# Packed attention and a gated feed-forward on one core: the first batch's attention with turned queries, scores in parts of the array and a block softmax on VectorE

## The chip, the cores and the metric

One core of one Trainium2 chip runs the whole program. The metric is the time of one execution on the device in microseconds (us), lower is better. The engines are named as the profile names them: PE is TensorE, DVE is VectorE, ACT is ScalarE, POOL is GpSimd and SP is SyncE, whose queue issues all loads and stores.

## What is computed

```python
q, k, v: (8, 8, 576, 64)   p: (8, 8, 32, 64)   w_in: (512, 2048)   w_out: (2048, 512)

def sm_attn(qq, kk, vv):
    s = scale * np.matmul(qq, kk.transpose(0, 1, 3, 2))
    s = s - np.max(s, axis=-1, keepdims=True)
    a = np.exp(s)
    a = a / (np.sum(a, axis=-1, keepdims=True) + 1e-09)
    return np.matmul(a, vv)
p_packed = sm_attn(p, k, v)                # 32 packed rows attend to 576 keys
out = sm_attn(q, p_packed, p_packed)       # 576 queries attend to the 32 packed rows
x = out.transpose(0, 2, 1, 3).reshape(8 * 576, 512)
h = x @ w_in
g = h * np.clip(h + 3.0, 0.0, 6.0) / 6.0
return g @ w_out
```

q, k, v and p arrive as 32-bit floats, the two weights as 64-bit floats, which the kernel reads as pairs of 32-bit words.

## The kernel before

Attention and feed-forward are done batch by batch, 576 rows each. The second attention's weights `a` (576 queries by 8 heads of 32) are never multiplied with the packed values. Instead the packed values are multiplied with w_in, which gives `m` for each strip `f` of 128 hidden columns (16 strips), and the hidden row is `a` times `m`. Numbers that must keep their precision are split into a rounded part `hi` and the remainder `lo`, and a product is then three matmuls: hi with hi, lo with hi, hi with lo.

For one strip f, first_moe does this: `gemm1` (12 matmuls into `h`), an activation on ACT (`t`, L954), the gate on DVE (L955), the rounding to `gh` on ACT (L963), the remainder `gl` on POOL (L965), and twelve matmuls of `second_product` (L856) into four accumulators, one strip later.

The weights of a strip come as 64-bit floats and are narrowed in a chain of four: two activations on ACT (L142, L144), a shift on DVE (L148), an addition on POOL (L152). w_in(f) is then ready for `m`; w_out(f) goes on to a rounding `wo_hi` on ACT (L162) and a remainder `wo_lo` on DVE or POOL (L164). The raw weights have two buffers for each matrix, and a buffer is free for the next load when POOL has added.

The first batch's attention (`first_attention`) has nothing to lie behind, so its pieces are written out by hand as generators, and `step` and `rest` move each on by one or more of its `yield`s: `b0` and `b1` are the second scores, softmax and split of head group 0 and 1 (`s2`), `m0` and `m1` are m of strip 0 and 1, `win0`, `wout0`, `win1`, ... are the narrowings. The order in which these calls stand is the order of the instructions on PE, DVE, ACT and POOL, and each engine works its queue strictly in that order. This holds for the attention of the first batch and for strips 0 to 3 of the feed-forward; after that a scheduler sets the order. `warm(n)` issues n matmuls on zeros whose result nobody reads.

In `s2` before, the queries are the stationary operand: the scores of 128 queries stand on 128 partitions with 32 packed rows of each head side by side. The softmax runs along the free axis straight from PSUM (L663, L666, L667, L670), and PE then turns the weights (L692, L695) into PSUM, from where ACT rounds them to `a_hi` (L698) and DVE takes the remainder `a_lo` (L701).

## Time and profile before

| | |
|---|---|
| three timed runs | 761.15, 763.76, 763.96 us; median 763.76 us |
| the profiled execution | 758.97 us, of which 757.1 us from the first to the last instruction |
| busy in the span | PE 98%, ACT 51%, DVE 44%, POOL 37% |
| instructions | 13994 |

A busy time is the time in which an engine works on something; matmuls overlap each other, and their ends are modelled. The granted clock is the share of full speed that TensorE was given. The two levels are 2.4 GHz (1.0) and 1.2 GHz (0.5).

### The profile page before, as it was taken

To read this page: it belongs to the slowest core of one execution; us is meant where nothing else is said; L and a number is where in the kernel's file an instruction comes from. 1 tells how busy PE (TensorE), PEld (TensorE's weight loads), DVE (VectorE), ACT (ScalarE), POOL (GpSimd) and SP (SyncE) were. 2 spreads that over 40 slices of the span, in tenths; PEclk is the share of its full clock that TensorE was granted. 3 is DMA by queue.
4 is the path that set the end of the run, shared out by engine and by line. 5 is a ranking of instruction groups with operands and counts; after the bars stand their busy time and mean duration, and the time that the engine had idled before them with its cause. 6 is when DMAs were issued, how large, how long until landed. Compare 5 with 4: busy or idle time off the path is not lost.

```text
span 757.1 us, 13994 instructions
## 1 busy us (share of the span) xinstructions
PE 739.4 (98%) x5197; PEld 583.4 (77%) x5197; DVE 336.3 (44%) x709; ACT 387.6 (51%) x922; POOL 282.3 (37%) x420
## 2 busy tenths in 40 slices
PE   8998898999999999999999999999999999999998
PEld 6775675768777877888777886788787887888886
DVE  3676648432463355342733446342643527321121
ACT  4677864644455446463455535463354635553343
POOL 0487973423233233332333223333333333343332
PEclk9999899999999999999999999999999999999999
DMA  9859983104420532043310524024220210000010
GB/s 257 261 144 218 237 223 63 56 9 88 102 37 29 103 67 52 1 88 71 63 43 1 114 53 82 1 58 98 47 61 1 61 33 29 1 29 0 2 42 29
DMA packets 191205, 55.98 MB, mean 74 GB/s; under 512 B 173216, under 2 KB 184480, under 8 KB 191136
## 3 DMA queue, kind: packets, MB, share of 16 engines
q1 hardware_dynamic: 191136, 55.08, 31.6%
q8 instruction: 41, 0.67, 0.4%
q14 instruction: 28, 0.23, 0.1%
HBM read 45.61 MB, written 9.44 MB: 73 GB/s over the span
## 4 chain that ended last, share of the span: by engine, by line
PE 83%; DMA 5%; DVE 4%; SPq 3%; ACT 3%; issue 1%; POOL 1%; DVEq 0%; POOLq 0%; ACTq 0%
PE acc L856 47%; PE ps_hh L827 23%; PE ps L268 6%; SPq L216 2%; DMA raw_in<-in_moe_w_in_dram 2%; PE ps L323 2%; DMA nat<-in_k_dram 1%; PE ps_h L451 1%; DVE tr L401 1%; PE ps L307 1%; SPq L254 1%; POOL x_out L152 1%; PE ps_w L639 1%; DMA raw_out<-in_moe_w_out_dram 1%; DMA spare<-in_k_dram 1%
## 5 line engine op out<-in xcount | busy, mean ns | idle before, releaser
L845 POOL TENSOR_TENSOR g<-t,g 128x256 fp32r<-128x256 f32 x224 | 167.5, 751 | 410.7 <-ACT g L844 384.5
L856 PE MATMUL acc<-wo_hi,g 128*128 128x512 f32 x896 | 316.4, 394 | 1.3 <-ACT g L844 1.3
L840 DVE SCALAR_TENSOR_TENSOR t<-t,ps_hh 128x320 f32<-128x320 f32 (+1 forms) x224 | 100.1, 449 | 251.8 <-ACT t L839 251.6
L839 ACT ACTIVATE t<-ps_hh,three 128x320 f32<-128x320 f32 (+1 forms) x224 | 112.4, 503 | 177.9 <-PE ps_hh L827 169.8
L856 PEld LDWEIGHTS acc<-wo_hi,g 128*128 128x128 f32 x896 | 167.7, 188 | 35.4 <-issue 3.5
L856 PE MATMUL acc<-wo_lo,g 128*128 128x512 f32 x448 | 177.6, 396 | 0.0
L844 ACT CAST g<-t 128x256 fp32r<-128x256 f32 x224 | 90.4, 405 | 93.9 <-DVE t L840 92.6
L827 PE MATMUL ps_hh<-a_hi,m_hi 128*128 128x320 f32 (+1 forms) x448 | 136.2, 304 | 0.3 <-DVE t L840 0.3
L827 PE MATMUL ps_hh<-a_lo,m_hi 128*128 128x320 f32 (+1 forms) x448 | 132.7, 296 | 0.0
L827 PE MATMUL ps_hh<-a_hi,m_lo 128*128 128x320 f32 (+1 forms) x448 | 132.7, 296 | 0.0
L827 PEld LDWEIGHTS ps_hh<-a_hi,m_hi 128*128 128x128 f32 x448 | 84.4, 188 | 34.4 <-issue 19.9
L856 PEld LDWEIGHTS acc<-wo_lo,g 128*128 128x128 f32 x448 | 84.5, 189 | 12.4 <-issue 2.1
L827 PEld LDWEIGHTS ps_hh<-a_lo,m_hi 128*128 128x128 f32 x448 | 84.5, 189 | 8.2 <-issue 0.9
L827 PEld LDWEIGHTS ps_hh<-a_hi,m_lo 128*128 128x128 f32 x448 | 84.5, 189 | 1.6 <-issue 1.3
L401 DVE STREAM_TRANSPOSE tr<-nat 128x576 f32<-128x576 f32 x56 | 41.8, 765 | 30.2 <-DMA nat<-in_q_dram 12.8
L391 DVE TENSOR_TENSOR m_lo<-ps,m_hi 128x512 fp32r<-128x512 f32 x56 | 36.1, 684 | 35.1 <-ACT m_hi L390 35.1
L851 POOL TENSOR_TENSOR bnd_lo<-t,bnd_hi 128x64 fp32r<-128x64 f32 x112 | 39.1, 349 | 0.0
L390 ACT CAST m_hi<-ps 128x512 fp32r<-128x512 f32 x56 | 30.0, 589 | 9.9 <-PE ps_hh L827 8.1
L268 PE MATMUL ps<-w_in_sb,pps 64*32 64x512 f32 x448 | 34.3, 601 | 0.6 <-DVE m_lo L391 0.6
L856 PE MATMUL acc<-wo_hi,gh 128*128 128x512 f32 x64 | 26.7, 417 | 2.7 <-ACT gh L963 2.7
L152 POOL TENSOR_TENSOR w_in_sb<-w_in_sb,raw_in 128x512 int32<-128x512 int32 x14 | 18.9, 1347 | 27.7 <-ACT raw_in L144 19.2
L965 POOL TENSOR_TENSOR gl<-t,gh 128x512 fp32r<-128x512 f32 x16 | 22.0, 1373 | 17.6 <-ACT bnd_hi L964 11.0
(171 smaller groups left out, 861.5 us busy)
## 6 DMA issues: line engine op xcount, KB each, us to landing
out_dram<-osb SPq DMA_DIRECT2D x36, 256.0 KB, 2.1
nat<-in_k_dram SPq DMA_DIRECT2D x112, 72.0 KB, 2.6
nat<-in_q_dram SPq DMA_DIRECT2D x112, 72.0 KB, 2.5
raw_in<-in_moe_w_in_dram SPq DMA_DIRECT2D x14, 512.0 KB, 5.6
raw_out<-in_moe_w_out_dram SPq DMA_DIRECT2D x14, 512.0 KB, 6.0
v_nat<-in_v_dram SPq DMA_DIRECT2D x56, 128.0 KB, 2.9
spare<-in_k_dram SPq DMA_DIRECT2D x2, 512.0 KB, 4.8
raw<-in_moe_w_in_dram SPq DMA_DIRECT2D x2, 512.0 KB, 4.4
```

Source lines behind the costliest of these rows:

```text
L152: nc.gpsimd.tensor_tensor(out=xi, in0=xi, in1=low, op=ALU.add)
L268: nc.tensor.matmul(banks[x][NPK * a:NPK * a + NPK, :n], rows[half, a], c, start=True, stop=True)
L390: nc.scalar.copy(out=hi[:, x], in_=ps)
L391: nc.vector.tensor_sub(out=lo[:, x], in0=ps, in1=hi[:, x].bitcast(F32))
L401: nc.vector.transpose(out=t, in_=state.pop(("nat", which, b, a)))
L827: nc.tensor.matmul(h[:, :n], mm[:, g, fs], aa[:, t0:t0 + n], start=(g == 0 and i == 0), stop=(g == NG - 1 and i == 2),)
L839: nc.scalar.activation(out=t[:, :n], in_=h, func=AF.Relu, bias=three)
L840: nc.vector.scalar_tensor_tensor(out=t[:, :n], in0=t[:, :n], scalar=6.0, in1=h, op0=ALU.min, op1=ALU.mult)
L844: nc.scalar.copy(out=gh, in_=tm)
L845: nc.gpsimd.tensor_sub(out=gl, in0=tm, in1=gh.bitcast(F32))
L851: nc.gpsimd.tensor_sub(out=bnd_lo[:, slot:slot + REM], in0=tb, in1=bh.bitcast(F32))
L856: nc.tensor.matmul(acc, gg, ww[:, f], start=(f == 0 and i == 0), stop=(f == NF - 1 and i == 2),)
```

## The change

The second scores of the first batch are computed the other way round. The packed values are the stationary operand, in pieces of 64 rows by 32 columns of the array (`products`, which the first scores use too), and the turned queries stream. The queries are turned by PE transposes in pairs of blocks, as the keys are, in place of matmuls with the identity; the last 64 queries of all heads come in one load and are turned together (`turn_rest`). The packing product `pack` writes 32 columns at a time. The softmax then works on blocks of 32x32: DVE transposes the scores from PSUM into `z`, takes maximum, difference, sum and reciprocal there, ACT the exponential, and DVE turns the blocks back into `at`. For group 0 POOL multiplies by the reciprocal and takes the remainder `a_lo`; for group 1 DVE does both. The narrowings stand at other places: those of strip 2 are no longer begun in first_attention, and in first_moe at f = 0 they follow the gate. The warm-up matmuls are 3, 7, 4, 3 in place of 3, 2, 2, 1, 3.

```diff
-WARM = (3, 2, 2, 1, 3)
+WARM = (3, 7, 4, 3)
...
@@ turned
-            for c in range(4):
-                for h in range(2):
-                    nc.tensor.matmul(
-                        ps[64 * h:64 * h + 64, c * P:(c + 1) * P], nat[:, h, c], ident, start=True, stop=True
-                    )
+            for j in range(4):
+                nc.tensor.transpose(
+                    out=ps[:, j * P:(j + 1) * P],
+                    in_=nat[:, j // 2, 2 * (j % 2):2 * (j % 2) + 2].rearrange("p c d -> p (c d)"),
+                    identity=ident,
+                )
...
+        def products(w, g, rows, blocks, cols, col_rest):
             s, sr = w[:, :, :2 * P], w[:, 0, 2 * P:2 * P + REM]
             for h in range(4):
                 for x in range(2):
+                    half = slice(64 * x, 64 * x + 64)
                     nc.tensor.matmul(
+                        s[32 * h:32 * h + 32, x], rows[half, 4 * g + h], cols[h // 2][half, h % 2], start=True, stop=True
                     )
             for x in range(2):
                 nc.tensor.matmul(
+                    sr[64 * x:64 * x + 64], blocks[:, 2 * g + x], col_rest[:, 2 * g + x], start=True, stop=True
+                )
+            return s, sr
...
@@ pack
-                for x in range(2):
+                for h in range(4):
                     nc.tensor.matmul(
-                        ps[64 * x:64 * x + 64],
-                        l[:, 64 * x:64 * x + 64],
-                        vt[x][:n, :, c],
+                        ps[NPK * h:NPK * h + NPK],
+                        l[:, NPK * h:NPK * h + NPK],
+                        vt[h // 2][:n, h % 2, c],
...
@@ s2
+            s, sr = products(wide(), g, pp, pp_bd, qt[2 * g:2 * g + 2], qtr)
+            yield
+            z = ap.tile([P, T, NPK], F32, name="z", tag="e", bufs=4)
+            flat = z.rearrange("p t n -> p (t n)")
+            for o, src in ((0, s[:, 0]), (2 * P, s[:, 1]), (4 * P, sr)):
+                nc.vector.transpose(out=flat[:, o:o + src.shape[1]], in_=src)
+            yield
+            mx = sm.tile([P, T], F32, name="mx2")
+            nc.vector.reduce_max(out=mx, in_=z, axis=AX.X)
+            yield
+            nc.vector.tensor_sub(out=z, in0=z, in1=mx.unsqueeze(2).to_broadcast([P, T, NPK]))
+            nc.scalar.activation(out=z, in_=z, func=AF.Exp, scale=scale)
+            yield
+            den = sm.tile([P, T], F32, name="den2")
+            nc.vector.reduce_sum(out=den, in_=z, axis=AX.X)
             nc.vector.tensor_scalar_add(den, den, 1e-9)
             nc.vector.reciprocal(den, den)
+            (nc.vector if g else nc.gpsimd).tensor_mul(
+                out=z, in0=z, in1=den.unsqueeze(2).to_broadcast([P, T, NPK])
+            )
+            yield
+            at = ap.tile([P, S], F32, name="at", tag="e", bufs=4)
...
+            nc.vector.transpose(out=at, in_=flat)
+            state["hi"] = nc.scalar.copy(out=hi, in_=at)
+            yield
+            state["lo"] = (nc.vector if g else nc.gpsimd).tensor_sub(out=lo, in0=at, in1=hi.bitcast(F32))
...
@@ first_attention, its end
+        rest(m0)
+        step(wout0, 3)
+        step(win1, 2)
+        step(b1)
+        step(wout0)
+        step(wout1, 2)
+        rest(win1)
+        step(b1)
         warm(WARM[1])
         h = ps_h0.tile([P, 2, 512], F32, name="ps_h0", tag="w")
         gemm1(h, 0, 0)
-        step(b1, 4)
+        rest(b1)
+        step(m1, 2)
         warm(WARM[2])
+        gemm1(h, 0, 1)
+        rest(m1)
+        rest(wout0)
         warm(WARM[3])
-        return h, {2: win2}, {1: wout1, 2: wout2}
+        return h, {1: wout1}
...
@@ first_moe, around the activation and the gate
-            step(in_(f + 2), 4)
+                step(in_(f + 2), 4)
...
             if f:
                 rest(m_(f + 1))
+            else:
+                step(in_(f + 2), 4)
             rest(out_(f + 1))
-            step(out_(f + 2), 3 if f else 1)
+            step(out_(f + 2), 3)
```

How the queues stand, at three places. On DVE, the softmax of group 0, from the second scores to the reciprocal, before:

```order
L663 TENSOR_REDUCE mx_332<-ps_w 128x16
L663 TENSOR_REDUCE mx_332<-ps_w 64x4
L666 TENSOR_TENSOR z_330<-ps_w,mx_332 128x512
L666 TENSOR_TENSOR zr_331<-ps_w,mx_332 64x128
L627 TENSOR_SCALAR pn<-ps_w,rinv 128x128
L148 TENSOR_SCALAR w_in_sb_321<-raw_in 128x512
L349 COPY pp_bd<-ps_t 64x2x32 x2
L670 TENSOR_REDUCE dn_333<-z_330 128x16
```

and in the changed kernel, on to the turning back of group 0:

```order
L623 TENSOR_SCALAR pn<-ps_w,rinv 128x128
L633 STREAM_TRANSPOSE z<-ps_w 128x256 x2
L633 STREAM_TRANSPOSE z<-ps_w 128x64
L636 TENSOR_REDUCE mx_349<-z 128x18
L148 TENSOR_SCALAR w_in_sb_353<-raw_in 128x512
L348 COPY pp_297<-ps_t 128x128
L351 COPY pp_bd<-ps_t 64x2x32
L638 TENSOR_TENSOR z<-z,mx_349 128x576
L642 TENSOR_REDUCE den_387<-z 128x18
...
L633 STREAM_TRANSPOSE z<-ps_w 128x256 x2
L633 STREAM_TRANSPOSE z<-ps_w 128x64
L636 TENSOR_REDUCE mx_396<-z 128x18
L638 TENSOR_TENSOR z<-z,mx_396 128x576
L653 STREAM_TRANSPOSE at<-z 128x576
```

The scaling of group 1's packed values (`pn`) now stands ahead of the first work on group 0's scores, and the turning back of group 0 (`at`) stands behind the transposes, maximum and difference of group 1.

On ACT, from the first activation of the feed-forward (strip 0) to the rounding of its gate, before:

```order
L954 ACTIVATE t<-ps_h_456,three 128x576
L162 CAST wo_hi<-x_out 128x512
L963 CAST gh<-t 128x512
L964 CAST bnd_hi<-t 128x64
```

and in the changed kernel, where raw_138 is w_in(2) the first time and w_out(2) the second, and L162 is w_out(1):

```order
L909 ACTIVATE t<-ps_h_444,three 128x576
L142 ACTIVATE raw_138<-raw_138 128x512
L144 ACTIVATE raw_138<-raw_138 128x512
L162 CAST wo_hi<-x_out 128x512
L142 ACTIVATE raw_138<-raw_138 128x512
L144 ACTIVATE raw_138<-raw_138 128x512
L920 CAST gh<-t 128x512
L921 CAST bnd_hi<-t 128x64
```

Four narrowing activations, which stood ahead of strip 0's activation, now stand between it and `gh`.

On POOL, from group 0's product with the reciprocal to the remainder `gl` of strip 0, before:

```order
L680 TENSOR_TENSOR zr_331<-zr_331,dn_333 64x128
L683 TENSOR_TENSOR z_330<-z_330,dn_333 128x256 x2
L152 TENSOR_TENSOR x_out<-x_out,raw_out 128x512
L652 MEMSET dn_431 128x4
L680 TENSOR_TENSOR zr_429<-zr_429,dn_431 64x128
L152 TENSOR_TENSOR x_out<-x_out,raw_out 128x512
L152 TENSOR_TENSOR w_in_sb_321<-w_in_sb_321,raw_140 128x512
L965 TENSOR_TENSOR gl<-t,gh 128x512
```

and in the changed kernel, where the additions are, in order, w_out(0), w_in(1), w_in(2) and w_out(1):

```order
L645 TENSOR_TENSOR z<-z,den_387 128x576
L656 TENSOR_TENSOR a_lo<-at,a_hi 128x576
L152 TENSOR_TENSOR x_out<-x_out,raw_out 128x512
L152 TENSOR_TENSOR w_in_sb_353<-w_in_sb_353,raw_in 128x512
L152 TENSOR_TENSOR w_in_sb_353<-w_in_sb_353,raw_138 128x512
L152 TENSOR_TENSOR x_out<-x_out,raw_out 128x512
L922 TENSOR_TENSOR gl<-t,gh 128x512
```

The remainder of group 0 is new there, the addition of w_in(1) has moved behind it (it stood ahead of the product with the reciprocal), and w_out(1) has moved behind w_in(2).

On PE, the last products of first_attention in the changed kernel stand as m of strip 1 (L196), four warm-up matmuls, then group 1's share of strip 0's gemm1; before, m of strip 1 stood ahead of group 0's share.

## Rows read from the trace of the kernel before

**Rows 1.** Busy time of each engine in three stretches: the first attention, the first feed-forward, the other batches.
```profile
0.00:37.00 37.00, 33.16 (x301) 25.40 (x301) 20.10 (x55) 20.39 (x45) 9.14 (x20) 1.00 0.88 262
37.00:110.00 73.00, 67.53 (x480) 51.10 (x481) 44.54 (x78) 56.51 (x114) 58.51 (x52) 0.95 0.88 206
110.00:757.00 647.00, 638.69 (x4418) 506.88 (x4417) 271.63 (x577) 310.75 (x764) 214.70 (x350) 1.00 0.23 48
```
Columns: stretch, its length, then busy us (and instructions) of PE, PE's weight loads, DVE, ACT and POOL, the granted clock, the share of the DMA engines, GB/s.

**Rows 2.** The chain of work that ended last, in order of time: start, length, what.
```profile
34.29 0.60 DVE wo_lo L164
...
85.40 1.07 PE ps L323 x40
```

**Rows 3.** PE in order of time, the first 30 us: start, length of the merged group, line, tile, shapes, number of records (a matmul of 32-bit floats leaves two records, a transpose one).
```profile
10.59 0.72 PE L568 MATMUL ps_w<-kt,pt 64*32 64x256 f32 x16
11.23 0.34 PE L576 MATMUL ps_w<-ktr,p_bd 128*64 128x64 f32 x4
...
12.26 1.05 PE L540 MATMUL ps_t<-ident,q_nat 128*64 128x128 f32 x16
13.62 0.66 PE L607 MATMUL ps_t<-ident,e 128*128 128x128 f32 x4 [0.31 <-ACT e L591]
...
15.23 1.04 PE L619 MATMUL ps_w<-v_nat,et 128*64 128x128 f32 x16
...
18.09 1.10 PE L639 MATMUL ps_w<-pp_bd,qt 128*128 128x64 f32 x8 [0.26 <-DVE pp_bd L349]
...
21.92 1.09 PE L540 MATMUL ps_t<-ident,spare 128*64 128x128 f32 x16
...
27.19 0.66 PE L692 MATMUL ps_t<-ident,z 128*128 128x128 f32 x4
```

**Rows 4.** DVE in order of time, first 40 us; in square brackets its idle time before, and what ended it.
```profile
20.78 0.88 DVE L663 TENSOR_REDUCE mx<-ps_w 128x16 f32<-128x512 f32 x2 [0.28 <-PE ps_w L639]
...
24.91 0.28 DVE L674 RECIPROCAL dn<-dn 128x20 f32<-128x20 f32 x1
```

**Rows 5.** Groups of instructions by line, shapes apart, over the whole execution: busy us, mean ns of one. L359 to L381 are the softmax of the later batches, which has the form that the changed first batch has.
```profile
L965 POOL TENSOR_TENSOR gl<-t,gh 128x512 fp32r<-128x512 f32 x16 | 22.0, 1373 | 17.6 <-ACT bnd_hi L964 11.0 <-ACT gh L963 6.6
...
L359 DVE STREAM_TRANSPOSE z<-ps 128x288 f32<-128x288 f32 x28 | 11.6, 452 | 2.9 <-PE ps L268 2.9
...
L378 DVE STREAM_TRANSPOSE at<-z 128x576 f32<-128x576 f32 x14 | 10.5, 758 | 0.0
...
L367 DVE TENSOR_REDUCE mx<-z 128x18 f32<-128x576 f32 x14 | 9.8, 743 | 0.1
...
L381 ACT CAST a_hi<-at 128x576 fp32r<-128x576 f32 x14 | 9.5, 676 | 8.9 <-DVE at L378 8.9
...
L369 ACT ACTIVATE z<-z 128x576 f32<-128x576 f32 x14 | 9.2, 681 | 8.2 <-DVE z L368 8.2
...
L683 POOL TENSOR_TENSOR z<-z,dn 128x256 f32<-128x256 f32 x2 | 1.2, 609 | 0.0
```

**Rows 6.** All engines in order of time, around the first activation of the feed-forward.
```profile
33.80 0.49 DVE L701 TENSOR_TENSOR a_lo<-ps_t,a_hi 128x320 fp32r<-128x320 f32 x1 [0.30 <-ACT a_hi L698]
...
35.14 0.42 DVE L148 TENSOR_SCALAR w_in_sb<-raw 128x512 int32<-128x512 int32 x1
...
35.30 1.40 POOL L152 TENSOR_TENSOR x_out<-x_out,raw_out 128x512 int32<-128x512 int32 x1 [3.04 <-DMA p_nat<-in_p_dram]
35.31 0.74 ACT L954 ACTIVATE t<-ps_h,three 128x576 f32<-128x576 f32 x1 [1.55 <-PE ps_h L451]
...
36.67 1.30 POOL L152 TENSOR_TENSOR w_in_sb<-w_in_sb,raw 128x512 int32<-128x512 int32 x1
...
37.38 1.14 DVE L164 TENSOR_TENSOR wo_lo<-x_out,wo_hi 128x512 fp32r<-128x512 f32 x1 [0.54 <-ACT wo_hi L162]
...
37.92 0.67 ACT L142 ACTIVATE raw<-raw 128x512 f32<-128x512 f32 x1
...
37.95 1.71 POOL L965 TENSOR_TENSOR gl<-t,gh 128x512 fp32r<-128x512 f32 x1
...
38.44 1.51 DVE L148 TENSOR_SCALAR x_out<-raw 128x512 int32<-128x512 int32 x1
```

**Rows 7.** PE in order of time from 30 to 75 us, as in rows 3.
```profile
35.11 1.46 PE L725 MATMUL ps_t<-pps 128*128 128x256 f32 x6
...
38.67 0.66 PE L196 MATMUL ps<-w_in_sb,pp_bd 128*64 128x128 f32 x8
39.26 0.50 PE L856 MATMUL acc<-wo_hi,gh 128*128 128x512 f32 x1
...
47.72 0.29 PE L451 MATMUL ps_h<-a_hi,m_hi 128*128 128x288 f32 x1
...
74.70 0.49 PE L856 MATMUL acc<-wo_hi,gh 128*128 128x512 f32 x1 [2.29 <-ACT gh L963]
```

**Rows 8.** Three stretches of the first feed-forward, columns as in rows 1.
```profile
45.00:50.00 5.00, 4.83 (x32) 3.93 (x31) 3.10 (x5) 4.01 (x10) 3.82 (x5) 1.00 0.13 31
...
75.00:80.00 5.00, 5.00 (x27) 3.66 (x26) 3.62 (x12) 3.79 (x10) 4.96 (x5) 0.66 1.09 320
...
85.00:90.00 5.00, 4.60 (x58) 3.84 (x59) 3.50 (x7) 4.07 (x9) 4.77 (x5) 0.66 1.07 335
```

**Rows 9.** What PE waited for from 37 to 110 us: us in total, times, longest.
```profile
PE ps L323 <- ACT et L308: 2.0, 1, 2.0
```

More of the change, by code (lines that the diff above doesn't have):

```diff
@@ L504, in turn_k, with turn_rest @@
             return t
-        def turn_k_rest(nat):
+        def turn_rest(nat, copy):
             ps = tail()[:, :NPAIR * REM]
@@ L513, in turn_k_rest @@
                 )
-            t = gp.tile([P, NPAIR, REM], F32, name="ktr0", tag="osb", bufs=2)
-            nc.vector.tensor_copy(out=t.rearrange("p a r -> p (a r)"), in_=ps)
+            t = gp.tile([P, NPAIR, REM], F32, name="rest0", tag="osb", bufs=2)
+            copy(out=t.rearrange("p a r -> p (a r)"), in_=ps)
             return t
@@ L576, in s1 @@
                 nc.tensor.matmul(
-                    sr[64 * x:64 * x + 64], p_bd[:, 2 * g + x], ktr[:, 2 * g + x], start=True, stop=True
+                    sr[64 * x:64 * x + 64], blocks[:, 2 * g + x], col_rest[:, 2 * g + x], start=True, stop=True
                 )
+            return s, sr
+        def s1(g, kt):
+            s, sr = products(wide(), g, pt, p_bd, kt, ktr)
             mx = sm.tile([P, 2], F32, name="mx")
@@ L657, in s2 @@
-            n = (P, REM)
-            def across(t, j, w):
-                return t[:n[j], w].unsqueeze(2).to_broadcast([n[j], w.stop - w.start, NPK])
-            for j, (z, s, w) in enumerate(main):
-                nc.vector.reduce_max(out=mx[:n[j], w], in_=s, axis=AX.X)
-                yield
-            for j, (z, s, w) in enumerate(main):
-                nc.vector.tensor_sub(out=z, in0=s, in1=across(mx, j, w))
-                nc.scalar.activation(out=z, in_=z, func=AF.Exp, scale=scale)
+            s, sr = products(wide(), g, pp, pp_bd, qt[2 * g:2 * g + 2], qtr)
@@ L712, in first_attention @@
         q0, q1 = (
-            load_pair(q, a, ap.tile([P, 2 * NST * D], F32, name="q_nat0", tag="nat", bufs=2)) for a in range(2)
+            load_q(a, ap.tile([P, 2 * NST * D], F32, name="q_nat0", tag="nat", bufs=2)) for a in range(2)
         )
+        qr = gp.tile([P, H, D], F32, name="q_rest0", tag="g", bufs=4)
+        nc.sync.dma_start(out=qr[:REM], in_=q[0, :, 4 * P:].rearrange("h r d -> r h d"))
         v1 = [load_pair(v, 2 + a, spare(2, a)) for a in range(2)]
         load_w(0, ("in",))
-        q2, q3 = (load_pair(q, 2 + a, spare(3, a)) for a in range(2))
+        q2, q3 = (load_q(2 + a, spare(3, a)) for a in range(2))
         load_w(0, ("out",))
@@ L895, in moe, with first_moe @@
                 second(2)
-    def first_moe(h, w_in, w_out):
+    def first_moe(h, w_out):
         ahead = attention(1) if B > 1 else iter(())
-        accs, m0 = [], {}
+        accs, w_in, m0 = [], {}, {}
         def attend(f, n):
```

151 lines of the change are left out of this document (38 added, 113 removed).

## The prediction

> **What bounds the kernel now.** I read the busy time by stages first. From 110 us on PE is busy for 638.7 of 647 us [rows 1], and the change touches no instruction there; that stretch is taken as it is. What can move is the first 110 us: the first attention, where PE is busy for 33.2 of 37 us, and the first feed-forward, 67.5 of 73. The chain of work then says who sets the pace inside: up to 34 us it runs over PE with short turns over DVE and ACT, and from 34.29 us it leaves PE for the narrowing of the weights and comes back to PE for good only at 85.40 [rows 2]. So a change in the first attention is worth what it does to the moment at which strip 0 is activated on ACT (35.31 us [rows 6]) and to the queues on ACT, DVE and POOL behind it. Its worth is not the PE time that it saves.
>
> **What PE saves.** Turning one pair of query heads takes PE 1.05 us in sixteen records; four transposes of the same size take 0.66 [rows 3], 0.4 less, four times. The second scores of a group are two runs like L639's 1.10 with a short one for the last queries behind each, some 2.6; the new form is that of the first scores, 0.72 and 0.34 [rows 3], 1.0 with their overlap. 1.6 less, twice. Packing takes the form that u_pv has, 1.07 [rows 2], against 1.04 [rows 3] and a tail put at 0.2, 0.2 less, twice. The two turns of the weights (0.66 and the last queries, about 1.0 each) go. That is 1.6 + 3.2 + 0.4 + 2.0 = 7.2 us of PE, and six more warm-up matmuls at 1.46 / 3 [rows 7] take 2.9 of it back. The loads of the last queries become one in place of four; query turns start without a wait for a load [rows 3], so this counts as nothing, and the cover is that PE still has the first scores to do when they land.
>
> **What reaches the softmax of group 0.** I follow the queues as they stand, with the durations of the rows; along the queues before, the same sum puts strip 0's activation at 35.4 and its second product at 39.2, where the rows have 35.31 and 39.26 [rows 6, 7]. Packing of group 0 starts with its copies at 15.1 (15.23 before [rows 3]), the packed keys are on DVE's output at 17.5, the second scores run from 17.9 to 18.8, and the second packing ends at 19.9, 2 us before the old one, behind which PE took up the next queries at 21.92 [rows 3]. But DVE's first transposes of z stand behind the scaling `pn` of that packing: they begin at 20.25, and DVE began at 20.78 before [rows 4]. Of 2 us, 0.5 get through. Then DVE does more than before: transposes of 576 columns at 0.452 for 288 [rows 5], 0.9; the maximum, 0.74 [rows 5]; L148, 0.42 [rows 6]; two small copies, put at 0.25 each. The difference is due at 22.55. By then POOL has begun the addition of w_in(0), at 22.3 for 1.30 us. What that does is in rows 6: L148 takes 0.42 when it starts with POOL idle (35.14) and 1.51 when POOL is at work from 37.95 to 39.66; it ends 0.3 after POOL. L164 likewise is at 1.14 until POOL is done. So the difference ends at 24.2, 0.95 later than by its own 0.74. Exponential 0.68, sum 0.74 [rows 5], addition and reciprocal 0.28 each at most [rows 4]: 26.3, against 25.19 before [rows 4]. The half microsecond in hand has become 1.1 late.
>
> The other way round the rows show little: POOL's addition at 35.30 began inside the L148 of 35.14 and took 1.40 against 1.30, 0.1 more. So the sum lets DVE wait for POOL, at two places on the path (0.95 here, 0.74 below), and POOL not for DVE.
>
> The Trainium skill, "SBUF — State Buffer", section "SBUF: two separate sides", makes it a lock on a port pair of VectorE and GpSimd that whoever begins first holds for its whole instruction, with the other blocked. By that rule POOL's addition of w_in(2) in strip 0 would also wait, for the last 0.3 us of an L148, and the forecast would be 773.6; by the rows it is 773.3. With no such waits at all it would be 771.6.
>
> **To the activation of strip 0.** POOL's product with the reciprocal costs 0.609 for 256 columns, 1.37 for 576 [rows 5]: 27.7. On DVE, group 1's transposes, maximum and difference now stand ahead of the turning back of group 0, which ends at 29.4 (0.758 [rows 5]); before, PE turned z at 27.19 [rows 3]. ACT rounds to 30.1 (0.676), and POOL's remainder, 1.37 for 512 columns [rows 5] and 1.45 for 576, ends at 31.6. Then DVE's sum of group 1, whose exponential is ready at 29.5, stands behind the L148 of w_out(0). This waits for ACT's second activation of it, queued behind a_hi of group 0, until 30.7, and for POOL's remainder until 31.6: 31.9. Sum, two small steps and product (0.74, 0.5, 0.75) end at 34.0, L148 of w_in(1) 34.3, the turning 35.0, the rounding 35.7, the remainder 36.5. Before it ended at 34.29 [rows 6].
>
> PE does not go on even then. In its queue m of strip 1 and four warm-ups stand ahead of group 1's share of gemm1, and m of strip 1 needs POOL's addition of w_in(1), now the third behind the remainder and w_out(0): 34.35 to 35.65. m takes 0.66 [rows 7], to 36.4; four warm-ups at 1.46 / 3 with overlap 1.85, to 38.2; six products 0.95, to 39.2. Strip 0's activation comes at 39.2 in place of 35.31: **3.9 late**.
>
> **Strip 0 of the feed-forward.** Before, `gh` stood on ACT behind one L162, whose w_out(1) POOL had begun to add at 35.30 [rows 6]. Now ACT has, behind the activation (0.74): two activations for w_in(2) at 0.67, done at 41.1. DVE's L148, 41.6. POOL's addition of w_in(2), 43.0, and only then that of w_out(1), 44.3 (1.30 and 1.40 [rows 6]). ACT's L162 waits for it, 44.9, then two more activations, 46.1, and `gh`, 46.6. What waits is PE's second product of strip 0: 46.7 in place of 39.26 [rows 7], after an idle of 3.0 us. `gl` on POOL follows `gh` and ends at 48.1, and the nine products left go on from there. Strip 1 runs with the queues as before; gemm1 of strip 3 starts at 55.7 in place of 47.72 [rows 7]: **8.0 late**. From there ACT and POOL stand to PE as they did before, so the rest shifts by 8.0. The cover that could eat this is loading: DMA was at 0.13 of its engines between 45 and 50 us [rows 8], so the weights were not waiting for bandwidth but for POOL to free their buffers, and POOL is late by the same 8.
>
> **The clock.** After PE's idle of 2.29 us before 74.70 [rows 7] and of 2.0 before the line at 85.4 [rows 2, 9] the granted clock has a mean of 0.66 over five microseconds, and 1.00 between [rows 8]: the lower level for part of it, (1 - 0.66) x 5 = 1.7 us lost each. The changed kernel idles on PE for 3.7 us (21.8 to 25.5: group 1's scores need the fourth query copy, which stands on ACT behind group 0's exponential), 3.3 (32.4 to 35.7) and 3.0 (43.7 to 46.7). The first is followed by work that has time. The second stands ahead of m and four warm-ups right on the path, the third ahead of the products. Bounds are 0 and 2 x 1.7 = 3.4; I take 1.5, less than half, since PE then waits for POOL again.
>
> **The sum.** 8.0 + 1.5 = 9.5 us on the profiled execution's 758.97, 768.5. The timed median is 763.76, 4.8 above the profiled one, and the forecast is made there: **773.3 us**. What POOL, DVE or ACT may differ by in their queues moves this by 2 either way.
>
> **Rivals.** (1) PE is what bounds the first attention: 33.2 of 37 us busy, and the chain up to 34 us on PE, speak for it. Then the 7.2 us less 2.9 come through, 4.3 faster, 759.5. It decides at one place: group 1's remainder must end before 34.3 and w_out(1) be added before strip 0's activation. The queues speak against both. So does DVE, where 2 us on PE have become 0.5. (2) The delay is eaten by the later stalls: 2.29 + 2.0 us of idle and 2 x 1.7 of clock, 7.7 in all, vanish if the weights' loads keep their times. 773.3 - 7.7 = 765.6, a difference that is hardly one. DMA at 1.07 to 1.09 from 75 us on [rows 8] speaks for it, the 0.13 at 45 us and the buffers that POOL frees late against it. (3) Only the first half happens: if w_out(1) is through in time, 3.9 + 1.5 remain, 769.2. It would need POOL to add it ahead of w_in(2), and it stands behind. (4) All three idles bring the clock down and more of DVE's work meets POOL's: 8.0 + 3.4 + 2, 777.2. (5) The parts of the array don't overlap, and 16 records take 1.3 us more: then group 0 starts 1.3 later, 774.6; the row at 10.59 speaks against it.
>
> **How the numbers follow.** A change of 0.5%, 3.8 us, is about what these runs tell from none. The forecast with (3) and (5), 769 to 776, has 0.68; (4) 0.14; (2) 0.12, of which most within 0.5%; (1) 0.06. The range is 765.5 to 778.5: it takes in (2) and (4), with a microsecond for the scatter of the timed runs, and leaves out (1) and the tails. Faster 0.06, the same 0.10, slower 0.84.
>
> **What would show it.** In the changed kernel's trace: DVE's transposes of z begin near 20.3 and its difference takes 1.7 us; strip 0's activation is at 38 to 40.5 us; between it and `gh` ACT waits for POOL's x_out; PE idles some 3 us ahead of its first second product; strip 3's gemm1 starts near 55.7 and everything after is shifted by that much; the granted clock falls at least once before 50 us. Wrong would be: `gh` within 3 us of the activation; PE busy without gaps from 20 to 37 us; or the two stalls near 75 and 85 us gone, which would give the loss back.

## The result, and the profile of the changed kernel

The changed kernel is slower: 766.78 us median of 12 runs (763.02 to 768.87) against 760.54 for the kernel before (12 runs, 757.93 to 763.96), a ratio of 1.0078 [1.0058, 1.0098]. Run again beside later experiments it gave 767.52 against 760.09, 1.0091 [1.0060, 1.0122]; one of its six runs there, 983.31 us at a granted clock of 0.676, is a slow one and is left out. The ratio compares the runs of a kernel with those of the kernel before taken beside them, with a 95% interval. By the ratios the change costs 5.9 and 6.9 us, by the medians 6.2 and 7.4. The forecast was 773.3, that is 9.5 more than a median of 763.76 for the kernel before. That median was of three runs; they are among the twelve above, whose median is 760.54. The profiled executions differ by 8.0: spans of 765.1 and 757.1. The one of before, on which the sum was built, is on the quick side, 758.97 us against medians of 760.54 and 760.09; that of the changed kernel, 766.90, is at its median.

The busy times by the stages of [rows 1], with the same columns:

```profile
0.00:37.00 37.00, 27.61 (x267) 19.31 (x268) 21.20 (x50) 16.79 (x36) 8.57 (x14) 0.91 0.93 260
37.00:110.00 73.00, 62.17 (x444) 47.66 (x444) 42.47 (x73) 53.17 (x107) 54.77 (x49) 0.95 0.76 182
110.00:765.00 655.00, 647.26 (x4471) 514.04 (x4471) 274.28 (x584) 317.19 (x776) 219.80 (x354) 1.00 0.23 50
```

PE is busy for 27.6 of the first 37 us, where it was 33.2. The work that the change takes from PE shows up as idle time: the first attention no longer has PE for its bound. PE's rows with the waits, the first and the second scores of group 0 ahead of them, then from the second scores of group 1 to the warm-ups behind m of strip 1:

```profile
10.06 0.66 PE L564 MATMUL ps_w<-kt,pt 64*32 64x256 f32 x16
...
16.64 0.67 PE L564 MATMUL ps_w<-qt,pp 64*32 64x256 f32 x16
...
22.16 0.64 PE L564 MATMUL ps_w<-qt,pp 64*32 64x256 f32 x8 [1.90 <-ACT qt L555]
23.21 1.08 PE L564 MATMUL ps_w<-qt,pp 64*32 64x256 f32 x8 [0.42 <-ACT qt L555]
...
30.19 0.40 PE L453 MATMUL ps_h<-a_lo,m_hi 128*128 128x288 f32 x1 [0.76 <-POOL a_lo L656]
...
33.83 1.12 PE L196 MATMUL ps_t<-w_in_sb,pp_bd 128*64 128x128 f32 x8 [2.70 <-POOL w_in_sb L152]
34.88 2.95 PE L683 MATMUL ps_t<-pps 128*128 128x256 f32 x8
```

and from m of strip 2 to gemm1 of strip 2, not every product shown:

```profile
42.08 0.66 PE L196 MATMUL ps<-w_in_sb,pp_bd 128*64 128x128 f32 x8
45.60 0.50 PE L811 MATMUL acc<-wo_hi,gh 128*128 128x512 f32 x1 [2.86 <-ACT gh L920]
...
46.97 0.71 PE L811 MATMUL acc<-wo_hi,gl 128*128 128x512 f32 x1 [0.64 <-POOL gl L922]
47.48 0.63 PE L811 MATMUL acc<-wo_hi,gh 128*128 128x512 f32 x1
47.90 0.63 PE L811 MATMUL acc<-wo_lo,gh 128*128 128x512 f32 x1
...
50.72 0.39 PE L811 MATMUL acc<-wo_hi,gl 128*128 128x512 f32 x1
50.94 0.29 PE L453 MATMUL ps_h<-a_hi,m_hi 128*128 128x288 f32 x1
```

All three predicted idles are there (1.90, 2.70, 2.86 us), and behind each PE runs at the lower clock for a while: eight short products of group 1's second scores take 1.08 in place of 0.64, m of strip 1 takes 1.12 against 0.66 in the row at 42.08, four warm-ups 2.95 against 1.99 (third experiment), and the second products stand 0.42 apart (47.48 to 47.90), where the last stands 0.22 ahead of what follows it. The mean granted clock over 45 to 50 us was 0.71; before it was 1.00 there [rows 8].

DVE's and POOL's rows say why the softmax took the time that it did. DVE first, from the transposes of group 0 to the remainder of group 1:

```profile
18.91 0.90 DVE L633 STREAM_TRANSPOSE z<-ps_w 128x256 f32<-128x256 f32 x3
...
21.18 0.74 DVE L638 TENSOR_TENSOR z<-z,mx 128x576 f32<-128x576 f32 x1
...
24.75 0.91 DVE L633 STREAM_TRANSPOSE z<-ps_w 128x256 f32<-128x256 f32 x3 [0.77 <-PE ps_w L568]
...
28.16 0.41 DVE L148 TENSOR_SCALAR x_out<-raw_out 128x512 int32<-128x512 int32 x1
...
29.27 0.91 DVE L643 TENSOR_SCALAR den<-den 128x18 f32<-128x18 f32 x1
...
30.51 1.50 DVE L645 TENSOR_TENSOR z<-z,den 128x576 f32<-128x576 f32 x1
...
33.77 0.76 DVE L656 TENSOR_TENSOR a_lo<-at,a_hi 128x576 fp32r<-128x576 f32 x1 [0.74 <-ACT a_hi L654]
```

then POOL's, to the addition of w_out(1) in strip 0:

```profile
21.07 1.99 POOL L152 TENSOR_TENSOR w_in_sb<-w_in_sb,raw_in 128x512 int32<-128x512 int32 x1 [19.06 <-DVE w_in_sb L148]
...
28.71 1.43 POOL L656 TENSOR_TENSOR a_lo<-at,a_hi 128x576 fp32r<-128x576 f32 x1 [3.43 <-ACT a_hi L654]
30.10 1.29 POOL L152 TENSOR_TENSOR x_out<-x_out,raw_out 128x512 int32<-128x512 int32 x1
32.48 1.29 POOL L152 TENSOR_TENSOR w_in_sb<-w_in_sb,raw_in 128x512 int32<-128x512 int32 x1 [1.09 <-DVE w_in_sb L148]
40.66 1.37 POOL L152 TENSOR_TENSOR w_in_sb<-w_in_sb,raw 128x512 int32<-128x512 int32 x1 [6.88 <-DMA raw_in<-in_moe_w_in_dram]
41.98 1.28 POOL L152 TENSOR_TENSOR x_out<-x_out,raw_out 128x512 int32<-128x512 int32 x1
```

and ACT's three rows of strip 0:

```profile
38.66 0.74 ACT L909 ACTIVATE t<-ps_h,three 128x576 f32<-128x576 f32 x1 [3.29 <-PE ps_h L453]
...
43.30 0.62 ACT L162 CAST wo_hi<-x_out 128x512 fp32r<-128x512 f32 x1 [2.76 <-POOL x_out L152]
...
44.94 0.60 ACT L920 CAST gh<-t 128x512 fp32r<-128x512 f32 x1
```

Executions begin their first scores at different moments, 10.59 us in the profiled one of before [rows 3] and 10.06 in that of after, as the first loads come. Counted from there, strip 0's activation is 3.88 us late (24.72 before, 28.60 after), its first second product 6.87 (28.67, 35.54), gemm1 of strip 3 8.89 (37.13; 56.08 in after, 46.02 from its scores).

### The profile page after: what moved, and what is told of

The parts are those of the page before. It is cut to its first block, busy times and chain, and to the rows that moved or that the text cites. A ratio compares the mean times of both kernels' runs of the same rounds, so it can differ in the third digit from the quotient of the medians.

```text
span 765.1 us, 13941 instructions
## 1 busy us (share of the span) xinstructions
PE 737.0 (96%) x5179; PEld 581.0 (76%) x5179; DVE 337.9 (44%) x707; ACT 387.2 (51%) x919; POOL 283.1 (37%) x416
## 4 chain that ended last, share of the span: by engine, by line
PE 82%; DMA 6%; DVE 3%; SPq 3%; ACT 3%; POOL 1%; issue 1%; DVEq 0%; POOLq 0%; ACTq 0%
PE acc L811 47%; PE ps_hh L782 23%; PE ps L268 6%; DMA raw_in<-in_moe_w_in_dram 3%; DMA nat<-in_k_dram 1%; PE ps L323 1%; SPq L254 1%; DMA raw<-in_moe_w_out_dram 1%; SPq L216 1%; DVE tr L403 1%; PE ps_h L453 1%; PE ps L307 1%; POOL x_out L152 1%; DMA spare<-in_k_dram 1%; POOL w_in_sb L152 1%
```

## The experiments

The same points for every kernel, as us later than in the kernel before (each counted from its own first scores, in its profiled execution), and the ratio to the kernel before, run beside it. Where a kernel was run twice, both values stand:

| kernel | activation 0 | second product 0 | gemm1 of strip 3 | median, us | ratio [95%] |
|---|---|---|---|---|---|
| changed | 3.9; 3.9 | 6.9; 6.9 | 8.9; 9.0 | 766.78; 767.52 | 1.0078 [1.0058, 1.0098]; 1.0091 [1.0060, 1.0122] |
| 1 narrowing ahead | 3.7 | 3.7 | 3.3 | 761.70 | 1.0019 [0.9996, 1.0043] |
| 2 no warm-ups behind m | 0.8 | 3.8 | 6.9 | 764.24 | 1.0061 [1.0039, 1.0083] |
| 3 w_in(1) first | 0.2 | 3.2 | 5.1 | 762.05 | 1.0036 [1.0021, 1.0051] |
| 4 before, narrowing behind | 1.1 | 4.1 | 7.3 | 763.09 | 1.0060 [1.0035, 1.0085] |
| 5 = 1 and 3 | 1.9 | 1.9 | 1.4 | 758.60 | 0.9990 [0.9975, 1.0005] |
| 6 warm-ups ahead of the product | 3.9; 5.3 | 6.9; 8.4 | 7.6; 9.1 | 765.80; 766.28 | 1.0078 [1.0057, 1.0099]; 1.0067 [1.0035, 1.0099] |
| 7 less on the chain | -1.8 | -0.8 | -0.2 | 758.05 | 0.9985 [0.9970, 1.0000] |
| 8 three idles filled | 0.2 | 3.2 | 4.0 | 761.55 | 1.0020 [1.0000, 1.0040] |
| 9 = 7, strips 0 and 1 in another order | -1.8 | -1.8 | 0.9 | 762.20 | 1.0027 [1.0003, 1.0052] |
| 10 = 9 mended | -1.8 | -1.8 | -2.1 | 758.26 | 0.9979 [0.9958, 1.0001] |

The kernel before alone has medians from 758.73 to 760.54 in the different sets of runs, so small gains are read from the ratios.

**1. The narrowing ahead of the activation again.**

```diff
         rest(wout0)
+        win2, wout2 = w_in_step(2), w_out_step(2)
+        step(wout1, 2)
+        step(win2, 2)
+        step(wout2, 2)
         warm(WARM[3])
...
```

In first_moe, strip 0 is ordered as in the kernel before.

> The changed kernel with one part undone: POOL's addition of w_out(1), two activations for w_in(2) and two for w_out(2) stand again ahead of strip 0's activation, where ACT is idle from 35.4 to 38.7 us, DVE from 36.4 and POOL from 33.8, and strip 0 is ordered as in the kernel before. Theory A (gh of strip 0 is late because it stands on ACT behind the cast of w_out(1), and that behind two additions on POOL): strip 0's activation stays near 38.7; gh follows within 2 us of it in place of 6.3; PE's waits of 2.86 and 0.64 us ahead of the first second products go, and with them the half clock on eight or so of the products (0.2 us each, 1.6); gemm1 of strip 3 starts 4 to 5 us earlier than 56.1, and the whole is faster than the changed kernel by 3.5 to 5 us, 762 to 763 us. Theory B (what is won here is given back, since later strips wait for their weights' loads): gemm1 of strip 3 moves by 4 us but the whole by less than 1.5. Theory C (the end of the attention alone makes the loss): less than 1.5 at strip 3.

Measured: 5.1 us faster than the changed kernel by the medians, 4.5 by the ratios. ACT's rows of strip 0:

```profile
38.86 0.74 ACT L913 ACTIVATE t<-ps_h,three 128x576 f32<-128x576 f32 x1 [1.76 <-PE ps_h L453]
...
40.42 0.62 ACT L922 CAST gh<-t 128x512 fp32r<-128x512 f32 x1 [0.32 <-DVE t L914]
```

`gh` follows the activation by 1.56 us in place of 6.28, and PE's first second product starts at 42.82 right behind m, with the others 0.23 apart in its trace. The activation itself has not moved. At strip 3 5.6 of the 8.9 us are gone. Theory A: a good half of the loss is this queue with the low clock behind its wait.

**2. Without the warm-ups behind m of strip 1.** `WARM = (3, 7, 0, 3)`.

> The changed kernel without the four warm-up matmuls between m of strip 1 and group 1's share of gemm1 of strip 0. Theory A (they are in the way: they run at the lower clock there, for 2.6 us, while the remainder of group 1 has been ready since 34.5): group 1's share starts at 35.0 in place of 37.5, itself at the lower clock and so 0.9 us longer; strip 0's activation at 37.0 to 37.3 in place of 38.66, all behind it as late as before against it; 1.3 to 1.7 us faster than the changed kernel. Theory B (they bring the clock back, and without them it stays low for longer): activation near 38, no gain, the half clock of the stretch lasts into strip 0. If what bounds the second product were something else than the queue behind the activation, it would not move.

```profile
32.77 0.66 PE L196 MATMUL ps_t<-w_in_sb,pp_bd 128*64 128x128 f32 x8 [2.38 <-POOL w_in_sb L152]
33.36 0.40 PE L453 MATMUL ps_h<-a_hi,m_hi 128*128 128x288 f32 x1
```

Measured: 2.5 us faster by the medians, 1.3 by the ratios, whose intervals overlap, so the gain of the whole is likely and not shown. On PE group 1's share now follows m at once, and the activation comes 3.1 earlier than in the changed kernel. That is twice what was expected, by luck: the clock fell at another moment in this execution, and m and the share ran at full speed. Of it 2.0 are left at strip 3, since PE idles as long as ever before the second product (2.87).

**3. w_in(1) ahead of w_out(0).**

```diff
-        step(wout0)
+        step(win1)
...
-        step(wout0, 3)
         step(win1, 2)
+        step(wout0, 2)
         step(b1)
-        step(wout0)
-        step(wout1, 2)
         rest(win1)
+        step(wout1, 2)
+        step(wout0, 2)
         step(b1)
```

> The changed kernel with the narrowing of w_in(1) ahead of that of w_out(0) on ACT, DVE and POOL, and no more work or less. Theory A (m of strip 1 is what PE waits 2.70 us for, since POOL adds w_in(1) third): POOL's addition of w_in(1) runs at 30.1 to 31.4 in place of 32.5 to 33.8; m of strip 1 starts at 31.4, PE's idle of 2.70 us shrinks to 0.3 and the clock does not fall there; group 1's share of gemm1 then waits for the remainder of group 1 alone, near 34.5; strip 0's activation at 35.5 to 36 in place of 38.66, and the whole 2.5 to 4 us faster than the changed kernel. Theory B (w_out(0), now late, is the next to hold ACT or DVE): the activation moves but the second product stays at 45.6 us or goes behind it. Theory C (DVE is the bound at the end of the attention, through what its operations wait for POOL): the remainder of group 1 ends later than 35.5 and the activation moves by less than 1.5.

```profile
23.96 0.91 DVE L633 STREAM_TRANSPOSE z<-ps_w 128x256 f32<-128x256 f32 x3 [0.17 <-PE ps_w L568]
...
30.68 0.66 PE L196 MATMUL ps_t<-w_in_sb,pp_bd 128*64 128x128 f32 x8 [0.34 <-POOL w_in_sb L152]
31.26 1.99 PE L683 MATMUL ps_t<-pps 128*128 128x256 f32 x8
...
41.73 0.50 PE L811 MATMUL acc<-wo_hi,gh 128*128 128x512 f32 x1 [2.87 <-ACT gh L920]
```

Measured: 4.7 us faster by the medians, 3.2 by the ratios. The idle of 2.70 is 0.34, the warm-ups take 1.99 in place of 2.95, the activation is as early as in the kernel before. The next idle, 2.87, is untouched. Theory A. Some 0.6 of the gain is luck: the idle ahead of group 1's second scores is there again (1.91 us), but the clock did not fall behind it, and DVE's transposes of these scores (the first row) begin 14.10 us behind the first scores, where the changed kernel has 14.69 (24.75).

**4. The kernel before with the new order of the narrowing.** The lines for w_in(2), w_out(2) and the last two steps of w_out(1) leave first_attention, and strip 0 is ordered as in the diff of the change.

> The kernel before with only the order of the narrowing around strip 0 changed as the changed kernel has it: POOL's addition of w_out(1) and the activations of w_in(2) and w_out(2) no longer stand ahead of strip 0's activation. Attention as before. Theory A (this order costs by itself what strip 0 loses): strip 0's activation stays at 35.3 us; gh comes 6 us behind it in place of some 3; the first second product starts at 42 to 43 in place of 39.26 after an idle of 2.5 to 3 us on PE; the granted clock falls there; the whole is 3 to 5 us slower than the kernel before. Theory B (these steps have other cover): within 1 us of the kernel before.

```profile
40.56 0.62 ACT L162 CAST wo_hi<-x_out 128x512 fp32r<-128x512 f32 x1 [2.79 <-POOL x_out L152]
...
42.21 0.61 ACT L961 CAST gh<-t 128x512 fp32r<-128x512 f32 x1
```

Measured: 2.9 us slower than the kernel before by the medians, 4.6 by the ratio. With the old attention untouched the same wait of 2.8 us stands on ACT and of 2.87 on PE. So this order costs by itself what strip 0 loses. The 1.1 by which the activation is late is something else: in this execution ACT waited 1.60 and 1.40 us for loads of w_in(0) and w_out(0), in that of before not at all and 0.64, and DVE's first maximum of group 0 stands behind them.

**5. The first and the third together.**

> The changed kernel with the edits of the first and the third experiment together: the narrowing of w_in(2), w_out(1), w_out(2) ahead of strip 0's activation, and w_in(1) ahead of w_out(0). Theory A (the end of the attention and the queue behind the activation are two separate delays, one behind the other): their gains add, 5.1 + 4.7 less the half clock that both won back (up to 1.7): 8 to 9.5 us faster than the changed kernel, 757.5 to 759; against the kernel before 1 to 2.5 us faster, since strip 0's activation comes at about the old time. Theory B (both remove the same wait): no more than 1 us better than the better of the two, 760.5 to 761.5. Theory C (the 7.2 us that PE saves in the attention come through once the two delays are gone): 755 to 756.

Measured: 0.9990 [0.9975, 1.0005], nothing left of the loss, nothing won either. Theory A with one addition: ACT now narrows up to 36.98, and the activation, whose products ended at 35.6, waits for it (1.9 late), which PE pays as an idle of 1.47 ahead of gemm1 of strip 1. PE's saving does not come through: theory C is out.

**6. Warm-ups in the wait of strip 0 alone.**

```diff
                 accs.extend(ps_o.tile([P, DM], F32, name="acc", tag="acc") for _ in range(4))
+                for _ in range(5):
+                    nc.tensor.matmul(accs[3][:, :2 * P], zeros[:, :P], zeros, start=True, stop=True)
```

> The changed kernel with five warm-up matmuls more on PE, between m of strip 2 and the first second product of strip 0, where PE waits 2.86 us; they end before the wait does. They do nothing for the output. Theory A (the wait brings the clock down, and that costs by itself): no fall of the clock there, the second products of strip 0 stand 0.23 us apart in place of 0.43 for eight of them, gemm1 of strip 2 starts 1.5 us earlier, and the whole is 1 to 2 us faster than the changed kernel. Theory B (the clock at this place costs nothing, since the strip behind waits for POOL and ACT anyway): the products run at full clock, but gemm1 of strip 3 moves by less than 0.5 us. Theory C: the five delay the product and the run is slower.

```profile
43.16 2.43 PE L866 MATMUL acc<-pps 128*128 128x256 f32 x10
46.12 0.50 PE L811 MATMUL acc<-wo_hi,gh 128*128 128x512 f32 x1 [0.53 <-ACT gh L922]
...
49.88 0.29 PE L453 MATMUL ps_h<-a_hi,m_hi 128*128 128x288 f32 x1
```

From the first second product to gemm1 of strip 2 it is 3.76 us in place of 5.34: at this place the clock costs 1.6. By the medians the whole is 1.0 faster than the changed kernel, by the ratios 0. Both were run once more, beside each other:

> The changed kernel once more, on the same chip as the runs beside it, so that gains of 1 to 2 us can be read against it: 5 to 7.5 us slower than the kernel before (6.2 by the first medians, 8.0 by the spans of the two profiled executions). If the 8.0 was the true size, the ratio comes out at 1.0105; if the profiled execution of before was a quick one, at 1.007 to 1.009.

> The sixth experiment once more beside the changed kernel itself, since by medians it showed 1.0 us and by ratios to the kernel before nothing. Theory A (the fall of the clock in strip 0 costs 1.5 us and the whole time follows): 1 to 2 us faster than the changed kernel of this call. Theory B (won in strip 0, given back later): within 0.7 us of it.

Measured: 766.28 against 767.52. Again 3.78 us between the same rows. But at strip 3 this second execution is no earlier than the changed kernel's (9.1 and 9.0): the clock stayed low for longer behind the idle ahead of m of strip 1, which put the activation 1.5 later than in the first. The gain of the whole, 1.0 and 1.2 by the medians, agrees with theory A, but the intervals of the ratios overlap, so it is shown in strip 0 and not for the whole. The changed kernel's own ratio leaves 5 to 9 us open, the 8.0 of the profiled pair within it.

**8. All three idles filled.** The five of the sixth, three warm-ups ahead of group 1's second scores, and the four of m ahead of it:

```diff
         step(tq[3])
+        warm(3)
...
+        warm(WARM[2])
         step(m1, 2)
-        warm(WARM[2])
```

> The changed kernel with warm-up matmuls in all three of PE's idle stretches: three ahead of group 1's second scores, the four that stood behind m of strip 1 now ahead of it, and five ahead of strip 0's first second product. Theory A (delay and clock are separate): granted clock 1.00 from 10 to 60 us; group 1's share of gemm1 right behind m of strip 1, strip 0's activation 2 to 2.5 us earlier, gemm1 of strip 3 4 us earlier than 56.1; 3 to 4 us faster than the changed kernel, so that some 3 us of its loss are the clock and warm-ups in the way, and the rest the queues. Theory B (idle is not what brings the clock down, or the clock costs nothing): no more than the second experiment gave, 1.3 to 2.5.

The windows of 20 to 37 and of 37 to 60 us (columns as in rows 1), in this kernel:

```profile
20.00:37.00 17.00, 13.23 (x87) 9.52 (x86) 14.25 (x28) 10.40 (x19) 7.31 (x6) 1.00 0.92 247
37.00:60.00 23.00, 21.59 (x129) 16.79 (x128) 14.26 (x23) 17.65 (x36) 17.76 (x16) 1.00 0.41 125
```

and in the changed kernel:

```profile
20.00:37.00 17.00, 11.22 (x64) 7.63 (x63) 13.00 (x25) 8.51 (x16) 7.12 (x5) 0.80 0.91 237
37.00:60.00 23.00, 19.18 (x107) 15.38 (x106) 11.62 (x19) 15.94 (x31) 14.69 (x14) 0.93 0.29 93
```

Measured: 6.0 us faster than the changed kernel beside it by the medians, 5.4 by the ratios, more than the 3 to 4 expected; 4.9 stand at strip 3. The clock is 1.00 throughout, and yet no queue of DVE, ACT or POOL was changed: in its trace PE still waits 0.53 us for `gh` and 0.64 for `gl`, behind the warm-ups. Two things are changed at once here. The four warm-ups no longer stand between m of strip 1 and group 1's share; at full clock they hold that place for 1.76 us (third experiment, 31.26 to the next product at 33.02). So some 1.8 of the 4.9 is their place in the queue, and the rest, about 3, the clock.

**7, 9, 10. A version faster than both?** The seventh takes group 1's last query copy from ACT to DVE, adds w_in(1) on POOL while DVE transposes, computes group 0's remainder on DVE while that waits for ACT, and narrows w_out(0) last.

> The fifth experiment's idea carried on, for a version that is faster than both kernels: the copy of the last queries of group 1 on DVE in place of ACT, where it stood behind the exponential of group 0; POOL's addition of w_in(1) while DVE turns and adds, that is out of the way of its products; the remainder of group 0 on DVE, in the gap in which it waits for the rounding of group 1; w_out(0) narrowed behind both; m of strip 1 and the warm-ups ahead of gemm1's first share; gh of strip 0 ahead of w_out(1)'s cast. Theory A (DVE's chain sets the end of the attention, and DVE loses 1.5 us there to POOL): the remainder of group 1 ends near 32 us in place of 34.5, strip 0's activation comes at 33 to 34, the first second product at 37 to 38; 9 to 11 us faster than the changed kernel, 2 to 4 faster than the kernel before. Theory B (PE is the next bound): activation not before 35, no better than the fifth experiment. Theory C (w_out(0) is late now): the second product stays near 39 to 40.

```profile
27.86 0.76 DVE L645 TENSOR_TENSOR z<-z,den 128x576 f32<-128x576 f32 x1
...
31.84 1.52 DVE L148 TENSOR_SCALAR w_in_sb<-raw 128x512 int32<-128x512 int32 x1
33.28 0.74 DVE L913 SCALAR_TENSOR_TENSOR t<-t,ps_h 128x576 f32<-128x576 f32 x1
```

The product with the reciprocal takes 0.76 in place of 1.50, and the activation comes 1.8 us earlier than in the kernel before. But an L148 of 1.52 stands ahead of strip 0's gate, and 0.2 is left at strip 3: 0.9985 [0.9970, 1.0000].

> The seventh experiment with the order of strips 0 and 1 mended: there DVE's L148 of w_in(2) met POOL's two additions and took 1.52 us ahead of strip 0's multiplication, and gl of strip 0 stood behind three additions on POOL. Now w_in(2) is added ahead of w_out(1), the L148 stands ahead of POOL's start, gl comes ahead of w_out(1)'s addition, and its cast and that of w_out(2) go behind the activation and gh of strip 1. Theory A: the multiplication starts 0.6 earlier, strip 0's second products have no wait, gemm1 of strip 2 starts 1.2 us earlier than in the seventh (40.4); 1 to 1.5 us faster than it, 1.5 to 3 us faster than the kernel before. Theory B (ACT, with five operations for weights in every strip, sets the pace of strips 1 to 3): the gain is gone by strip 3, the same as the seventh.

```profile
44.09 0.62 ACT L162 CAST wo_hi<-x_out 128x512 fp32r<-128x512 f32 x1 [3.41 <-POOL x_out L152]
```

A miss: 1.0027. The cast of w_out(2), moved behind `gh` of strip 1, waits 3.41 us on ACT, strip 2's activation stands behind it, and PE waits 3.02 for it ahead of gemm1 of strip 3. It is the changed kernel's own mistake two strips later.

> The seventh experiment with the order of strip 0 as in the ninth, and with the mistake of the ninth mended: there, PE waited 3.02 us ahead of gemm1 of strip 3 for strip 2's multiplication, since ACT's activation of strip 2 stood behind the late casts of w_out(2) and the narrowing of two more strips. Now, up to strip 4, w_out of a strip is cast in that strip, behind its activation, and that of the next one is narrowed there, so that no strip carries more than one cast. Theory A (it was this order): no wait above 0.5 us on PE between 30 and 60 us; gemm1 of strip 3 starts 1 us earlier than in the seventh (45.96), and the whole is 1 to 2 us faster than the kernel before or better. Theory B (the strips 5 and 6, which now get two casts at once, pay for it): the gain of strip 3 is gone by 80 us, as in the ninth, and the whole is within 0.2% of the kernel before or behind it.

```profile
79.19 0.61 PE L453 MATMUL ps_h<-a_hi,m_hi 128*128 128x288 f32 x1 [3.72 <-ACT m_hi L207]
```

Measured: 0.9979 [0.9958, 1.0001], 2.1 us ahead at strip 3, with no wait above 0.33 on PE between 30 and 60 us. Of theory B the loss came, a wait of 3.72 ahead of gemm1 of strip 7 after which 1.1 are left; that two casts make it is not shown, since ACT waited there 0.88 and 1.15 us for loads of weights, and seven of the other kernels wait 1.05 to 2.69 at the same place. Seven and ten tend to be 1 to 1.6 us faster than the kernel before; neither interval is clear of none.

## Why the prediction was right, and where it was wrong

**The mechanism was right.** Signs that came: idles on PE of 1.9, 2.7 and 2.9 us, ACT waiting for POOL's x_out between the activation and `gh`, strip 0's activation 3.88 late (forecast 3.9), the clock down before 50 us, gemm1 of strip 3 at 56.08 (55.7). Signs that did not: DVE's transposes of z began at 18.91 (forecast near 20.3), and its difference took 0.74 (forecast 1.7). The experiments show two separate delays: the third takes away the late end of the attention, the first the queue behind the activation, the fourth makes this queue in the kernel before, and the fifth, with both taken away, has nothing of the loss left. Rival (1), PE as the bound, fell with PE's idles and the fifth. Rival (3), the first half only, fell with PE's idle of 2.86, and rival (5), array parts that don't overlap, with group 0's second scores, sixteen records in 0.67 us. Of rival (4) the clock came, 3.2 of its 3.4 us (below), its further waits for POOL in part.

**The step that failed is the one from the profiled execution to the time.** "The timed median is 763.76, 4.8 above the profiled one, and the forecast is made there." The median of twelve runs is 760.54: the base was 3.2 too high, and that is half of the 6.5 us between 773.3 and 766.78, which lies inside the range, at its lower end. The other 3.3 is in the 9.5. This difference was worked out on one execution of 758.97, and by the twelve runs that execution was a quick one. Of the 8.9 that the changed kernel is late at strip 3, 7.9 are left between the times of the two profiled executions and 6.2 between the medians. On the base of the profiled execution the same sum gave 768.5, against 766.90 for the profiled execution of the changed kernel.

**The sum itself came near, 9.5 against 8.9 at strip 3, by two errors that cancelled.** It had 8.0 for the queues and 1.5 for the clock; the rows have about 5.7 and 3.2. That the activation came as late as forecast is luck of this kind.

*The delays were put too high.* "So the difference ends at 24.2, 0.95 later than by its own 0.74": it took 0.74. It began 0.11 us behind POOL's addition, and POOL was the one to lose time (1.99 in place of 1.30). By the rule of the Trainium skill, "SBUF — State Buffer", section "SBUF: two separate sides", whoever begins first has the ports for the whole instruction; by the starts in these rows that was POOL, yet DVE went through. The prediction had taken the one side from L148's rows, on a margin of a quarter microsecond, and had POOL never wait for DVE. The trace of before shows that it does, where DVE begins first (gl takes 1.28 us at 128.97):

```profile
133.85 0.72 DVE L383 TENSOR_TENSOR a_lo<-at,a_hi 128x576 fp32r<-128x576 f32 x1
...
133.97 1.76 POOL L965 TENSOR_TENSOR gl<-t,gh 128x512 fp32r<-128x512 f32 x1 [3.45 <-ACT gh L963]
```

The second place that the sum priced did not wait either. "This waits for ACT's second activation of it ... 31.9": L148 of w_out(0) ran at 28.16 in 0.41, ahead of that activation, since it needs only the first. Two operations that the sum has without a wait met POOL instead: the product with the reciprocal (1.50, ended 0.62 behind POOL) and L643 on 18 columns (0.91). The packing, too, was shorter than its price: 0.65 us for 32 records, where 1.07 came from a row behind a stall, in a stretch with a granted clock of 0.66 [rows 2, 8]. In the end the remainder of group 1 was there at 34.5 where the sum had 36.5, 1.5 us too late from the same first scores. m of strip 1 began at 33.83 where the sum had 35.65, 1.3 earlier from the same first scores, although 0.6 of low clock (below) stands ahead of it: the queues up to there were put 1.9 too high.

*The clock was put too low.* "I take 1.5, less than half, since PE then waits for POOL again." Up to strip 3 the changed kernel loses 0.6 on group 1's second scores (against the third experiment, where the clock did not fall there), 0.5 on m of strip 1 (1.12 against 0.66), 0.8 on the four warm-ups (2.60 from their first to the next product, against 1.76 in the third experiment) and 1.6 on the second products, of which 1.3 are left at strip 3 (sixth experiment): 3.2. The first three, 1.9, are why the activation still came as late as forecast. The 0.6 also answers "The first is followed by work that has time": DVE's chain of group 1 waits for those scores. And the argument for "less than half" fails where it stood: behind the second and the third idle PE has work lined up for as long as the clock is low, and of POOL it waits there only for `gl`, 0.64 us. The eighth experiment agrees: 3.2 of clock and 1.8 for the place of the warm-ups, and 4.9 came back.

*What follows strip 3.* The spans differ by 8.0: of the 8.9 0.5 is the earlier first scores of the one execution, and 0.4 was won back by its end. The medians differ by 6.2 and 7.4, since the profiled execution of before was 1.1 to 1.6 quicker than its medians, while the prediction added a difference from it to a median. Rival (2), the later stalls that give it back, named 765.6, nearer to the measured time than the forecast; but that rests on the base that was 3.2 too high, and the stalls are there again in the changed kernel, moved by 7 to 8 us, with one more at 89.07:

```profile
82.09 0.50 PE L811 MATMUL acc<-wo_hi,gh 128*128 128x512 f32 x1 [2.41 <-ACT gh L920]
...
89.07 0.40 PE L453 MATMUL ps_h<-a_hi,m_hi 128*128 128x288 f32 x1 [2.27 <-ACT m_hi L207]
...
93.23 0.90 PE L323 MATMUL ps<-v_nat,et 128*32 128x64 f32 x40 [1.56 <-ACT et L308]
```

against 2.29 at 74.70 and 2.0 at 85.4 before. A part of rival (2) did come: in the trace of before the clock falls behind both stalls [rows 8], in that of the changed kernel only behind the last (94.5 to 98.5 us), and in its second one behind neither. How much this gives back in the average run, and how much is scatter, stays open; one execution of before and two of the changed kernel are profiled.

## What to carry to other kernels

A change that relieves the busiest engine in a stretch of handovers was worth nothing by itself here; ask which queue hands over last, and what each step that was moved now stands in front of. A stretch of idle on TensorE can be paid twice, once as waiting and once as low clock on the work behind it: price the clock in full where PE has work lined up behind the wait, and expect it to vary, since the same idle brought the clock down in one execution and not in another. Filling the three idles, with the warm-ups moved off the path, gave back 4.9 us at strip 3, about as much as mending either queue (5.6 and 3.8). Set a sum made on one profiled execution against the times of many runs: first see where that execution lies among them, and don't take a median of three for the base.

## What the runs showed of the hardware

Which operations of DVE wait for POOL can be read from the rows. Beside a POOL addition that began 0.4 to 0.7 us earlier, DVE's additions and products of two operands in SBUF ended 0.55 to 0.62 us behind POOL's end, and its L148 some 0.28 behind it (L645 above, 1.50 in place of 0.76; L164 and L148 in [rows 6]); the gate, which reads PSUM, kept its 0.74 to 0.76. Where DVE began first, by 0.12 us, POOL took the longer time (1.76 in place of 1.28, in the trace of before above). Where DVE's difference began only 0.11 behind POOL, POOL lost the time, in the changed kernel and in the third experiment alike (1.99 and 2.00 us); an L164 that began 0.12 behind (61.57 us in the changed kernel) took 1.73, and an L148 that began 0.08 behind (98.25 us) took 1.53. So close together the starts in a trace don't tell who waits. Warm-up matmuls on zeros kept the granted clock at 1.00 from 20 to 60 us (eighth experiment), where it had been 0.80 and 0.93. An idle does not bring it down every time: the 1.9 us ahead of group 1's second scores did in the changed kernel, and did not in the third and the seventh experiment.
